# Two loads of 2 KB rows for the key and value weights, a first token block in column halves, and another order of value segments, in an attention and gated-MLP kernel

## The chip, the cores and the metric

The kernel runs on one core of one Trainium2 chip. The metric is the device time of one execution in microseconds (us). Before the change its median was 267.1 us. The five executions behind it lie between 266.8 and 267.2 us, so that an effect of half a microsecond is near the edge of what times alone can show. The profile's span (first to last instruction of the program) is about 2 us shorter than the device time.

PE is TensorE, PEld its weight loads, DVE is VectorE, ACT is ScalarE, POOL is GpSimd, SP is SyncE.

## The reference, cut to what matters

```python
def reference(A_x, A_wqkv, A_wo, B_x, B_w_gate, B_w_up, B_w_down):   # S = 2048, D = 512, F = 1792, bf16
    xn = _layernorm(A_x)
    # A: 32 heads of 16, causal sliding window of 256
    q, k, v = split(xn @ A_wqkv)
    p = softmax(where(mask, q @ k.T * Dh ** -0.5, -1e9))
    # B: (xn @ w_gate) * (xn @ w_up) @ w_down
    return A_x + (p @ v) @ A_wo + ((xn @ B_w_gate) * (xn @ B_w_up)) @ B_w_down
```

`B_x` isn't used. The work is cut into 4 chunks of 512 tokens, and a chunk into 4 token blocks of 128.

## The kernel before

The kernel plans itself: a small model in Python decides in which order instructions are issued and on which engine an evacuation runs; constants such as `land` and `wq` tell that model when loads land. They are not waits. In the traces each engine follows its list and waits on semaphores. An evacuation is the copy of a result of PE out of its accumulation memory; a load's landing is the time of the semaphore event that completes it.

The loads of the first chunk. Token block 0 comes from two queues, block 1 from ACT's, and then the weights in three loads of 512 KB each with rows of 1 KB: values, keys, queries.

```python
        load(nc.sync, self.x[0:64, 0, :], xv[0:64, 0, :])
        load(nc.scalar, self.x[64:128, 0, :], xv[64:128, 0, :])
        load(nc.scalar, self.x[:, 1, :], xv[:, 1, :])
        for n, lo in enumerate((1024, 512, 0)):
            load(nc.sync, self.Wqkv[:, :, lo:lo + 512], w["qkv"][:, :, lo:lo + 512])
            if n:
                load(nc.sync, self.x[:, n + 1, :], xv[:, n + 1, :])
        # ... then gate, up, the other tokens, down, output weights
```

A token block b of the first chunk goes: statistics (DVE), square root (ACT), reciprocal and "apply" (DVE), turn (four 128x128 transposes on PE), copy of the turned block to `xnT` (ACT or DVE), then projections on PE: values `v0.b`, keys `k0b<b>`, queries `q0b<b>`. PE's order before (warm-ups are matmuls on a constant whose results nobody reads; the gate group is the first work of part B):

```
42 warm-up matmuls, turn0, 6 warm-ups, v0.0, turn1, k0b0, k0b1, q0b0, q0b1, turn2, v0.1, v0.2, turn3, k0b2, q0b2, k0b3, q0b3, first gate group ...
```

The value groups (probabilities times values), 4 in each chunk. A segment is one strip of probabilities; each is eight small matmuls with 17 weight columns each, side by side in the array, which stream 64*m columns, m from 1 to 5. Long and short segments alternate:

```python
    def i_values(self, T, c, strips, banks):
        rest = sorted(((P, s) for P, batch in strips for s in batch), key=lambda x: -x[1][2])
        segments = []
        while rest:
            segments.append(rest.pop(0))
            if rest:
                segments.append(rest.pop())
        for n, (P, (k, q, m, at)) in enumerate(segments):
            # ... for lane in 2: for e in 4: one matmul of 64*m columns into banks[lane]
```

In chunks 1 to 3 that is m = 5,1,5,1,5,2,5,2,4,3,4,3 (96 matmuls), in chunk 0 it is 5,1,5,1,5,2,4,3,4 (72 matmuls).

The softmax here doesn't subtract the row's maximum and nothing guards it: scores larger than these inputs give would overflow.

## Time and profile before

| | before |
|---|---|
| median time | 267.1 us |
| span of the profile | 264.9 us |
| start to the first gate matmul | 17.51 us |
| from there to the end of the last vector addition | 244.44 us |
| from there to the end of the span | 3.00 us |

From the page of the kernel before: busy time and share, then busy tenths in 40 equal slices of the span, and what the DMA engines moved in each slice.

```profile
PE 260.4 (98%) x3458; PEld 131.0 (49%) x3458; DVE 190.1 (72%) x365; ACT 165.4 (62%) x122; POOL 119.2 (45%) x272
...
PE   8999999999999999999999999999999999999994
...
GB/s 188 373 374 351 226 43 0 4 2 0 4 2 32 90 22 24 0 2 2 2 0 42 83 22 20 0 6 0 2 2 22 21 22 22 0 2 0 2 2 80
```

PE is busy nearly always; the first slice (6.6 us) is the only one before the last that isn't full, and there the DMA engines move half of what they move in the next. Matmuls are pipelined and their ends modelled, so "busy" alone doesn't prove a limit. The waits of PE do (engine and line, what it waited for, us in total, times, longest; PEq is PE's own sequencer, at launch):

```profile
PE M L194 <- PEq L796: 0.8, 1, 0.8
PE M L669 <- ACT xnT L198: 0.2, 1, 0.2
```

Nothing else over 0.15 us in the whole program. The chain of waits of the first 20 us (start, us, what) is followed back from the end of that stretch ("issue" is time in which the profile shows nothing that was waited for):

```profile
0.84 4.64 PE M L194 x42
5.48 0.44 PE M L608 x4
5.92 0.02 issue
5.94 0.60 ACT xnT L198
6.55 0.04 issue
6.59 1.06 PE M L669 x16
7.66 0.33 PE M L608 x4
7.99 3.69 PE M L204 x64
```

Turn 0 at 5.3, its copy at 5.94, value projection 0 at 6.59, turn 1, then four projections of keys and queries without a gap. No DMA is in the chain. The landings, read from the trace's semaphore events: values 6.24 us, keys 7.73 (used at 7.82), queries 9.60 (used at about 9.7).

### The profile page before, as it was taken

What the parts mean: (1) busy time and instruction counts of PE and PEld (TensorE: products, weight loads), DVE (VectorE), ACT (ScalarE), POOL (GpSimd) and SP (SyncE); (2) the same over time, 40 slices, a digit from 0 to 9 for tenths busy, and PEclk for the clock granted to TensorE, in tenths of its full rate; (3) what the DMA queues carried; (4) which work ended last, traced back from release to release, by engine and by line L of the source; (5) the groups of instructions that cost most, each with busy time, mean ns of one, the idle gap of its engine ahead of it and who ended that gap; (6) DMA issues with size and microseconds to landing.
All of it is one profiled execution on the core that took longest, in us unless ns stands there. A gap on an engine that the chain in (4) does not pass through costs nothing.

```text
span 264.9 us, 7986 instructions
## 1 busy us (share of the span) xinstructions
PE 260.4 (98%) x3458; PEld 131.0 (49%) x3458; DVE 190.1 (72%) x365; ACT 165.4 (62%) x122; POOL 119.2 (45%) x272
## 2 busy tenths in 40 slices
PE   8999999999999999999999999999999999999994
PEld 8974444554445354464534353446544344544462
DVE  4889987888997629697996639796754449787404
ACT  3637676677677666777667676567886766673000
POOL 1404664554356463708256454718063545537000
PEclk9999999999999999999999999999999999999999
DMA  6999920000001300000001300000000000000002
GB/s 188 373 374 351 226 43 0 4 2 0 4 2 32 90 22 24 0 2 2 2 0 42 83 22 20 0 6 0 2 2 22 21 22 22 0 2 0 2 2 80
DMA packets 17251, 13.88 MB, mean 52 GB/s; under 512 B 7104, under 2 KB 17216, under 8 KB 17216
## 3 DMA queue, kind: packets, MB, share of 16 engines
q1 hardware_dynamic: 16848, 13.11, 17.3%
q8 instruction: 27, 0.44, 0.7%
q10 hardware_dynamic: 368, 0.26, 0.4%
q14 instruction: 8, 0.07, 0.1%
HBM read 9.70 MB, written 2.10 MB: 45 GB/s over the span
## 4 chain that ended last, share of the span: by engine, by line
PE 97%; DMA 1%; DVE 1%; ACT 0%; issue 0%
PE M L204 72%; PE S L212 9%; PE M L241 7%; PE M L669 6%; PE M L194 2%; DMA out_dram<-xn 1%; PE S L204 1%; DVE xn L762 1%; PE M L608 0%; ACT xnT L198 0%
## 5 line engine op out<-in xcount | busy, mean ns | idle before, releaser
L493 ACT ACTIVATE P<-S 128x2048 bf16<-128x2048 f32 x76 | 140.9, 1854 | 55.3 <-PE S L212 50.6
L221 POOL TENSOR_SCALAR_AFFINE_SELECT P<-P 64x256 bf16<-64x256 bf16 (+1 forms) x248 | 112.2, 455 | 117.4 <-ACT P L493 105.1
L204 PE MATMUL M<-xnT,Wg 128*128 128x512 bf16 x224 | 57.7, 380 | 0.0
L204 PE MATMUL M<-xnT,Wu 128*128 128x512 bf16 x224 | 57.7, 380 | 0.0
L204 PE MATMUL M<-Wd,hT 128*128 128x512 bf16 (+1 forms) x224 | 52.1, 373 | 0.0
L720 DVE TENSOR_TENSOR hT<-M,gsb 128x512 bf16<-128x512 f32 x56 | 38.2, 682 | 8.1 <-PE M L204 7.8
L204 PEld LDWEIGHTS <-hT 128*128 128x128 bf16 x238 | 21.7, 98 | 24.0 <-issue 2.8
L204 PEld LDWEIGHTS <-Wu 128*128 128x128 bf16 x224 | 20.5, 98 | 25.5 <-issue 2.8
L204 PEld LDWEIGHTS <-Wg 128*128 128x128 bf16 x224 | 20.1, 98 | 25.0 <-issue 3.5
L200 DVE CAST gsb<-M 128x512 bf16<-128x512 f32 x40 | 27.4, 686 | 5.3 <-PE M L204 5.0
L204 PE MATMUL M<-xnT,Wqkv 128*128 128x128 bf16 (+1 forms) x224 | 30.4, 288 | 0.0
L212 PE MATMUL S<-Q,K 32*128 32x320 bf16 (+3 forms) x720 | 30.0, 254 | 0.0
L227 DVE TENSOR_TENSOR P<-P,masks 128x512 int16<-128x512 int16 x56 | 22.6, 410 | 9.2 <-ACT P L493 9.2
L529 DVE STREAM_TRANSPOSE at<-M 128x512 f32<-128x512 f32 x32 | 21.4, 698 | 10.5 <-PE M L241 10.4
L212 PEld LDWEIGHTS <-K 32*128 32x128 bf16 x720 | 11.9, 92 | 32.3 <-issue 31.3
L280 DVE TENSOR_SCALAR K<-M,own 128x512 bf16<-128x512 f32 x28 | 20.0, 742 | 3.5 <-PE M L204 3.2
L204 PEld LDWEIGHTS <-Wqkv 128*128 128x128 bf16 x224 | 15.8, 98 | 10.8 <-issue 1.6
L241 PE MATMUL M<-P,V 64*17 64x320 bf16 (+4 forms) x1440 | 20.2, 252 | 0.0
L762 DVE TENSOR_TENSOR y<-M,x 128x512 bf16<-128x512 f32 x12 | 8.2, 684 | 15.0 <-PE M L204 14.9
L241 PEld LDWEIGHTS <-V 64*17 64x17 bf16 x1440 | 15.8, 85 | 2.8 <-issue 1.3
L204 PE MATMUL M<-Wo,OT 128*128 128x512 bf16 (+1 forms) x64 | 16.2, 374 | 0.0
L669 PE MATMUL M<-Wqkv,xnT 128*64 128x256 bf16 x256 | 15.7, 274 | 0.2 <-ACT xnT L198 0.2
(51 smaller groups left out, 136.2 us busy)
## 6 DMA issues: line engine op xcount, KB each, us to landing
Wg<-in_B_w_gate_dram SPq DMA_DIRECT2D x2, 896.0 KB, 10.3
Wu<-in_B_w_up_dram SPq DMA_DIRECT2D x2, 896.0 KB, 12.5
Wqkv<-in_A_wqkv_dram SPq DMA_DIRECT2D x3, 512.0 KB, 5.5
out_dram<-y SPq DMA_DIRECT2D x12, 128.0 KB, 1.7
x<-in_A_x_dram SPq DMA_DIRECT2D x1, 1024.0 KB, 14.3
Wd<-in_B_w_down_dram SPq DMA_DIRECT2D x2, 512.0 KB, 12.3
Wd<-in_B_w_down_dram SPq DMA_DIRECT2D x2, 384.0 KB, 8.5
x<-in_A_x_dram SPq DMA_DIRECT2D x1, 512.0 KB, 11.5
```

The lines of the kernel that those rows point to most:

```text
L200: self.nc.vector.tensor_copy(out=out, in_=in_)
L204: self.nc.tensor.matmul(ps, lhsT=a, rhs=b, start=first and n == 0, stop=last and n == len(pairs) - 1)
L212: self.nc.tensor.matmul(self.S[:, e, 64 * at:64 * (at + m)], lhsT=self.K[U % 3][rows, c, j].rearrange("p l t -> p (l t)"), rhs=self.Q[T % ...
L221: self.nc.gpsimd.affine_select(out=v, in_=v, pattern=[[0, 4], [0, n], [sign, 64]], base=0, fill=0.0, compare_op=ALU.is_gt if kind else ALU ...
L227: self.nc.vector.tensor_tensor(out=v, in0=v, in1=m, op=ALU.bitwise_and)
L241: self.nc.tensor.matmul(banks[lane][32 * e:32 * e + 17, 64 * q:64 * (q + m)], lhsT=self.V[U % 3][rows, j, 4 * c + e, 0:17], rhs=P[rows, e, ...
L280: self.nc.vector.tensor_scalar(out=out, in0=in_, scalar1=own, scalar2=None, op0=ALU.mult)
L493: ex = self.op(f"exp{g}", {"A": (took + 0.06, took + 0.18)}, [o], lambda e: self.nc.scalar.activation(out=P[:, :, 0:hi], in_=self.S[:, :, ...
L529: t = self.op(f"tr{v}", {"V": (0.63, 0.71)}, [o] + ts, lambda e, par=par: nc.vector.transpose(out=self.at[:, :, par, :], in_=self.M[banks[ ...
L669: self.nc.tensor.matmul(self.M[i][64 * lane:64 * lane + 64, 256 * jj:256 * jj + 256], lhsT=self.xnT[T % 2][:, k, tok], rhs=w[:, lane], sta ...
L720: x = self.op(f"u{T}.{f}", {"V": PSUM_COPY["V"]}, [o, ("gate", T, f)], lambda e: self.nc.vector.tensor_tensor(out=self.hT[T % 2][:, f, :], ...
L762: self.nc.vector.tensor_tensor(out=keep["y"][:, cols], in0=self.M[i][:, cols], in1=self.x[:, t, cols], op=ALU.add)
```

## The change

Its intent: get keys and values sooner by larger rows; start the first value projection on half of the columns while the other half is still being turned, copied and loaded; and order the value segments so that PE's instruction feed keeps up. The diff, cut to its core (a rank and the dependences that go with the halves are left out):

```diff
-    FIRST = True
+    FEED = 0.1
@@ loads
-        for n, lo in enumerate((1024, 512, 0)):
-            load(nc.sync, self.Wqkv[:, :, lo:lo + 512], w["qkv"][:, :, lo:lo + 512])
-            if n:
-                load(nc.sync, self.x[:, n + 1, :], xv[:, n + 1, :])
+        for k, cols in ((0, slice(512, 1536)), (2, slice(512, 1536))):
+            load(nc.sync, self.Wqkv[:, k:k + 2, cols], w["qkv"][:, k:k + 2, cols])
+        load(nc.sync, self.x[:, 2, :], xv[:, 2, :])
+        load(nc.sync, self.Wqkv[:, :, 0:512], w["qkv"][:, :, 0:512])
+        load(nc.sync, self.x[:, 3, :], xv[:, 3, :])
@@ value segments
-        rest = sorted(..., key=lambda x: -x[1][2])
-        segments = []
+        rest = sorted(..., key=lambda x: x[1][2])
+        keep, segments, t = rest.pop(0), [], 0.0
         while rest:
-            segments.append(rest.pop(0))
-            if rest:
-                segments.append(rest.pop())
+            fit = [n for n, x in enumerate(rest) if t + x[1][2] / 37.5 >= self.FEED * (len(segments) + 1)]
+            segments.append(rest.pop(fit[0] if fit else -1))
+            t += segments[-1][1][2] / 37.5
+        segments.append(keep)
@@ first chunk: what the planning model believes of the landings
-        land = (3.75, 3.9, 7.9, 9.8)
-        wv, wk, wq = 6.1, 7.4, 9.4
+        land = (3.6, 3.9, 7.3, 8.8)
+        wkv, wq = 6.3, 8.4
@@ block 0: apply, turn and copy in two column halves; 4 warm-ups after the turns, not 6
+            parts = 2 if b == 0 else 1
+            for n in range(parts):
+                cols = slice(n * 512 // parts, (n + 1) * 512 // parts)
 # ...
@@ value projection: weight rows outside, so that its first half needs rows 0 and 1 alone
-            for jj in range(2):
-                tok = slice(128 * b + 64 * jj, 128 * b + 64 * jj + 64)
-                for k in range(4):
+            for k in range(4):
+                for jj in range(2):
+                    tok = slice(128 * b + 64 * jj, 128 * b + 64 * jj + 64)
 # ... start=k + jj == 0, stop=k + jj == 4
```

With these constants the planner also gives PE another order in the first block:

```
... turn0 (two halves), 4 warm-ups, v0.0, k0b0, turn1, q0b0, k0b1, q0b1, turn2, ...
```

Value segments become 4,4,5,2,5,3,5,2,5,3,1,1 and, in chunk 0, 4,4,5,2,5,3,5,1,1.

More of the change, by code (lines that the diff above doesn't have):

```diff
@@ L229, in i_values @@
     def i_values(self, T, c, strips, banks):
-        rest = sorted(((P, s) for P, batch in strips for s in batch), key=lambda x: -x[1][2])
-        segments = []
+        rest = sorted(((P, s) for P, batch in strips for s in batch), key=lambda x: x[1][2])
+        keep, segments, t = rest.pop(0), [], 0.0
         while rest:
-            segments.append(rest.pop(0))
-            if rest:
-                segments.append(rest.pop())
+            fit = [n for n, x in enumerate(rest) if t + x[1][2] / 37.5 >= self.FEED * (len(segments) + 1)]
+            segments.append(rest.pop(fit[0] if fit else -1))
+            t += segments[-1][1][2] / 37.5
+        segments.append(keep)
         for n, (P, (k, q, m, at)) in enumerate(segments):
@@ L265, in i_root, with i_apply @@
                                      in1=self.mhalf[:, 0:n], op=ALU.pow)
-    def i_apply(self, t):
+    def i_apply(self, t, cols=slice(0, 512)):
         w, b = t // 4 % 2, t % 4
-        self.nc.vector.tensor_scalar(out=self.xn[b][:], in0=self.x[:, t, :], scalar1=self.mv[w][:, b, 0:1],
+        self.nc.vector.tensor_scalar(out=self.xn[b][:, cols], in0=self.x[:, t, cols], scalar1=self.mv[w][:, b, 0:1],
                                      scalar2=self.rs[w][:, b:b + 1], op0=ALU.subtract, op1=ALU.mult)
@@ L583, in bn @@
                 nc.vector.bn_aggr(out=self.mv[0][:, b, :], in_=keep["st"][:])
-            s = self.op(f"st{b}", {"V": (0.92, 0.94)}, [land[b]] + applied * (b == 1 and self.FIRST), bn, rank=3 + b)
+            s = self.op(f"st{b}", {"V": (0.92, 0.94)}, [land[b]] + applied * (b == 1), bn, rank=0.5)
             s = self.op(f"sq{b}", {"A": (0.20, 0.25)}, [s], lambda e, b=b: nc.scalar.activation(
@@ L590, in first_chunk @@
                 out=self.rs[0][:, b:b + 1], in_=self.ve[:, b:b + 1]), rank=0)
-            applied = [self.op(f"ap{b}", {"V": (0.38, 0.48)}, [s], lambda e, b=b: self.i_apply(b), rank=0)]
-            self.at_["ap", b] = applied[0]
-        self.op("table", {"A": (1.5, 1.5)}, roots, lambda e: nc.scalar.activation(
+            parts = 2 if b == 0 else 1
+            for n in range(parts):
+                cols = slice(n * 512 // parts, (n + 1) * 512 // parts)
+                took = (0.38, 0.48) if parts == 1 else (0.22, 0.30)
+                self.at_["ap", b, n] = self.op(f"ap{b}", {"V": took}, [s], lambda e, b=b, cols=cols: self.i_apply(b, cols), rank=0)
+            if b == 0:
+                applied = [self.at_["ap", 0, 1]]
+        self.op("table", {"A": (1.5, 1.5)}, roots + [("Q", 0, 0, 2)], lambda e: nc.scalar.activation(
             out=self.warm[:], in_=self.warm[:], func=ACT.Exp), rank=1)
-        last = self.op("masks", {"V": (0.15, 0.2)}, [self.at_["ap", 1]], lambda e: nc.vector.memset(self.masks[:], -1), rank=9)
+        last = self.op("masks", {"V": (0.15, 0.2)}, [self.at_["ap", 1, 0]], lambda e: nc.vector.memset(self.masks[:], -1), rank=9)
         for n in range(5):
@@ L603, in first_chunk, with turn, turned @@
             tok = slice(128 * b, 128 * b + 128)
-            ap = self.at_["ap", b]
-            def turn(i, b=b):
-                for k in range(4):
+            def turn(i, ks, b=b):
+                for k in ks:
                     self.nc.tensor.transpose(self.psT(i)[:, k, :], self.xn[b][:, 128 * k:128 * k + 128], self.ident[:])
                 if b == 0:
-                    self.keep_busy(6, 3)
-            def turned(o, i, b=b, tok=tok):
-                x = self.op(f"xT{b}", {"A": (0.48, 0.6), "V": (0.31, 0.41)}, [o],
-                            lambda e: self.copy(e, self.xnT[0][:, :, tok], self.psT(i)), rank=0)
+                    self.keep_busy(2 * ks[0], 3)
+            def turned(o, i, ks, b=b, tok=tok):
+                took = {"A": (0.48, 0.6), "V": (0.31, 0.41)} if len(ks) == 4 else {"A": (0.27, 0.38)}
+                ks = slice(ks[0], ks[-1] + 1)
+                x = self.op(f"xT{b}", took, [o], lambda e: self.copy(e, self.xnT[0][:, ks, tok], self.psT(i)[:, ks]), rank=0)
                 self.frees(x, i)
-                self.at_["xnT", 0, b] = x
+                self.at_["xnT", 0, b] = self.at_["xnT", 0, b, ks.start] = x
+                x.then.append(lambda o: self.at_.update({("begun", 0, b, ks.start): o.start}))
             def project(i, lo, tok=tok):
@@ L639, in first_chunk @@
             at = len(self.A) - 2 if b else 0
-            self.A.insert(at, Dense(f"turn{b}", 1.1, [ap], turn, turned))
-            self.add_v(0, b, wv)
-            self.add(f"k0b{b}", 4.2, [("xnT", 0, b), wk], lambda i, f=project: f(i, 512), k_out)
+            for n, ks in enumerate(([0, 1], [2, 3]) if b == 0 else ([0, 1, 2, 3],)):
+                self.A.insert(at + n, Dense(f"turn{b}", 1.1 * len(ks) / 4, [("ap", b, n)], lambda i, f=turn, ks=ks: f(i, ks),
+                                            lambda o, i, f=turned, ks=ks: f(o, i, ks)))
+            self.add_v(0, b, wkv - 0.6)
+            self.add(f"k0b{b}", 4.2, [("xnT", 0, b), wkv], lambda i, f=project: f(i, 512), k_out)
             self.add(f"q0b{b}", 4.2, [("xnT", 0, b), wq], lambda i, f=project: f(i, 0), q_out)
@@ L663, in emit @@
         def emit(i):
-            for jj in range(2):
-                tok = slice(128 * b + 64 * jj, 128 * b + 64 * jj + 64)
-                for k in range(4):
+            for k in range(4):
+                for jj in range(2):
+                    tok = slice(128 * b + 64 * jj, 128 * b + 64 * jj + 64)
                     w = self.Wqkv[:, k, 1024:1536].rearrange("p (h l d) -> p l h d", l=2, d=16)
@@ L669, in emit @@
                         self.nc.tensor.matmul(self.M[i][64 * lane:64 * lane + 64, 256 * jj:256 * jj + 256],
-                                              lhsT=self.xnT[T % 2][:, k, tok], rhs=w[:, lane], start=k == 0,
-                                              stop=k == 3, tile_position=(0, 64 * lane), skip_group_check=True)
+                                              lhsT=self.xnT[T % 2][:, k, tok], rhs=w[:, lane], start=k + jj == 0,
+                                              stop=k + jj == 4, tile_position=(0, 64 * lane), skip_group_check=True)
         def evac(o, i):
@@ L677, in evac @@
             self.at_["V", T, b] = x
-        self.add(f"v{T}.{b}", 4, [("xnT", T, b), land] + self.ring(T, 2)[:1 if T == 3 else 0], emit, evac, "C")
+        x = [("xnT", T, b)] if T + b else [("xnT", 0, 0, 0), ("begun", 0, 0, 2)]
+        self.add(f"v{T}.{b}", 4, x + [land] + self.ring(T, 2)[:1 if T == 3 else 0], emit, evac, "C")
     def add_qk(self, T, c):
```

## The prediction

> **What bounds the kernel.** TensorE. The page gives PE 260.4 us of a 264.9 us span (98%), PE is 97% of the chain of waits, and its only waits over 0.15 us are 0.8 us at launch and 0.2 us before the first value projection. From 6.59 to about 258.8 us PE always has a matmul in flight. So only two things can pay: real work starting before 6.59 us, and less time per PE group. The order of instructions, compared without lines and bank numbers, is the same in both programs after the first token block, apart from the value segments.
>
> **First block.** Before (timeline): 42 warm-up matmuls fill PE until 5.27 us, four turns start there, the ACT copy runs 5.94 to 6.54 (0.60), values start at 6.59, the next turn at 7.59. The weights landed at 6.24 (values), 7.73 (keys), 9.60 (queries). After:
> - The first apply, halved, ends near 5.0, but the turns still wait for the warm-ups at 5.27: nothing gained.
> - The first half copy can start near 5.70 and takes about 0.39 (estimate: 0.60 less half of the streaming). Values' first half starts near 6.1, its second near 6.5, once the second copy and rows 2, 3 of the weights are in. Gain about 0.45 us.
> - Loads: in the DMA view 1 KB packets take about 65 ns in the first microseconds and 45 ns from 6 us on. Rows of 2 KB halve the packets of 1 MB. "DMA: Bandwidth & Descriptors" of the Trainium skill (Why small descriptors are slow) gives a fixed cost per packet; this trace does not show what a 2 KB packet takes early. I take the new landing constants of the diff as a guess: keys and values near 6.5, queries near 8.6.
> - Then PE does key projection 0 (0.92), turn 1 (0.23) and reaches query projection 0 near 8.25, before its weights. I expect a new wait of 0.3 to 0.4 us there, which gives most of the 0.45 back. Net 0.1 to 0.45, taken as 0.25 us.
>
> **Value groups.** Each of the 12 groups with 96 matmuls takes 1.27 us up to the next group's start, of the 4 with 72 0.98 us (PE timeline). Streaming alone, 64 columns in about 28 ns, is 1.07 and 0.80. In the first 32 matmuls starts are 3 to 4 ns apart within a segment; the fifth segment's are 8 ns apart, its eighth 29 to 55 ns late, and this lag stays until the end. "TensorE: Matmul & The Clock Gate" (Architectural detail) gives a PE queue of 64, which is 32 pairs of load and matmul: it fits the place of the stall. Order 5,1,5,1 streams those 32 in 0.34 us, the new one (4,4,5,2,5,3,5,2,5,3,1,1) in 0.41 us, so the queue should be refilled in time. Estimate 0.03 to 0.06 us a group, 16 groups: 0.5 to 0.95, taken as 0.75 us.
>
> Value projections only swap loop order: 58 ns a matmul as before.
>
> **Prediction.** 267.1 - 0.25 - 0.75 = 266.1 us; 265.2 to 266.8. Faster by over 2%: 0.01; within 2%: 0.98; slower: 0.01.
>
> **What would show it.** Values from about 6.1 us; a PE wait for a DMA near 8.3 us; turn 2 at 11.1 to 11.4 instead of 11.51; value groups at about 1.21 and 0.93 us; dense groups unchanged (0.86 to 0.96); the tail after the last value group still about 19 us.
>
> **What would make it wrong.** 2 KB rows that land no earlier; the feed not limiting the groups; the PE clock rising later with fewer warm-ups; the score stage waiting for the query copy that moves from ACT to DVE.

## The result, and the profile after

267.0 us (266.92 to 267.61, 5 runs), against 267.1 us before. The ratio is 1.0006, with a 95% interval of 0.9991 to 1.0021. (A ratio here is the mean time of one kernel's runs over the mean of the other's runs of the same rounds, so not quite the ratio of the medians.) Executions over 1.5% slower than the fastest of the same kernel are left out of the means. A second series, 6 runs on another chip, gave 266.78 us against 267.34 and 0.9987 (0.9973 to 1.0000). So one series shows a loss of 0.16 us and the other a gain of 0.35 us, neither of them clear of nothing, where a gain of 1.0 us was predicted; the first lies just above the stated range of 265.2 to 266.8 us.

| part of the span, us | before | again | changed | again |
|---|---|---|---|---|
| start to the first gate matmul | 17.51 | 17.91 | 18.14 | 17.93 |
| to the last vector addition | 244.44 | 244.42 | 243.83 | 243.83 |
| to the end | 3.00 | 3.00 | 3.00 | 3.00 |

The middle part won 0.61 us and repeats within 20 ns. The start lost 0.63 us between the first traces; from trace to trace it varies by 0.4 us for before and by 0.2 us for the changed kernel.

The page of the changed kernel, lines as before:

```profile
PE 259.0 (98%) x3456; PEld 131.1 (49%) x3456; DVE 189.7 (72%) x367; ACT 165.0 (62%) x122; POOL 119.9 (45%) x272
...
PE   7899999999999999999999999999999999999994
...
GB/s 201 378 377 349 205 43 0 4 0 2 4 2 20 101 22 24 0 2 2 2 0 42 82 21 22 0 6 0 2 2 22 20 24 22 0 2 0 2 2 80
```

PE works 1.4 us less and is idle in the second slice too. The DMA engines moved 201 GB/s in the first slice, not 188: 7% more, no more than that. The waits of PE in the changed kernel:

```profile
PE M L679 <- DMA Wqkv<-in_A_wqkv_dram: 0.7, 1, 0.7
PE M L614 <- DVE xn L271: 0.6, 1, 0.6
PE M L205 <- DMA Wqkv<-in_A_wqkv_dram: 0.2, 1, 0.2
```

The DVE wait is the turns' for the apply; they begin at 5.27 us as before. The two waits for `Wqkv` are new: the second half of value projection 0 waits for the second load of keys and values, and query projection 0 for the query weights. PE's timeline (start, us, engine, line, operation, tiles, shape, count, and in brackets what ended the idle time before it):

```profile
6.03 0.63 PE L679 MATMUL M<-Wqkv,xnT 128*64 128x256 bf16 x8
7.37 0.63 PE L679 MATMUL M<-Wqkv,xnT 128*64 128x256 bf16 x8 [0.71 <-DMA Wqkv<-in_A_wqkv_dram]
7.93 1.07 PE L205 MATMUL M<-xnT,Wqkv 128*128 128x128 bf16 x16
8.84 0.39 PE L614 MATMUL M<-ident,xn 128*128 128x128 bf16 x4
9.46 2.85 PE L205 MATMUL M<-xnT,Wqkv 128*128 128x128 bf16 x48 [0.24 <-DMA Wqkv<-in_A_wqkv_dram]
```

The values did start at 6.03 us, 0.56 earlier. Their second half ran at 7.37, when the second load landed (7.33). So they end at 7.93, 0.34 later than before. And query projection 0, which is now one projection earlier in PE's order, met the landing of its weights (9.41). The chain of waits of the first 20 us now goes through that landing:

```profile
3.32 6.10 DMA Wqkv<-in_A_wqkv_dram
9.41 0.05 issue
9.46 2.85 PE M L205 x48
```

PE by stretches, before and then changed: us of the stretch, PE busy, count, PEld busy (the rest is DVE, ACT, POOL, clock, DMA share and GB/s).

```profile
6.59:17.51 10.92, 10.92 (x189) 10.34 (x190) 9.53 (x22) 5.71 (x11) 2.97 (x12) 1.00 1.07 372
17.51:261.95 244.44, 243.91 (x3221) 115.33 (x3218) 177.84 (x334) 157.23 (x107) 115.17 (x251) 1.00 0.13 34
```

```profile
6.03:18.14 12.11, 11.16 (x189) 10.32 (x189) 9.88 (x24) 5.60 (x11) 3.07 (x12) 1.00 1.06 378
18.14:261.97 243.83, 243.29 (x3221) 116.70 (x3218) 177.13 (x335) 157.14 (x108) 115.75 (x251) 1.00 0.12 33
```

From the first value matmul to the first gate matmul the same PE work took 10.92 us before, without idle time, and 12.11 us now. That is the whole loss: PE began the block 0.56 us earlier and ended it 0.63 us later. Counted from start to start, the two waits cost more than the 0.71 and 0.24 us in the brackets, which leave out the tail of the matmul before: the second half of the values starts 1.34 us after the first half (before 0.46), and query projection 0 starts 0.62 us after turn 1 (before, what follows turn 1 starts after 0.23). That is 0.88 and 0.39 us.

The gain, in one value group of chunk 2 (PE's timeline, before and then changed; the time to read is from the start of the 96 matmuls to the start of the next line):

```profile
156.97 1.34 PE L241 MATMUL M<-P,V 64*17 64x320 bf16 x96
158.24 0.60 PE L204 MATMUL M<-Wo,OT 128*128 128x512 bf16 x2
```

```profile
157.30 1.29 PE L243 MATMUL M<-P,V 64*17 64x256 bf16 x96
158.52 0.60 PE L205 MATMUL M<-Wo,OT 128*128 128x512 bf16 x2
```

It takes 1.27 us before and 1.22 us after. All 16 groups together: 19.116 us before, 18.520 after, so 0.596 us less; 11 of the 12 long ones went from 1.27 (the last one from 1.25) to 1.22, the four short ones from 0.976 to 0.943, and one became longer (1.270 to 1.295, in the same place in every trace of the new order). In that one the 96 matmuls start as in the others, the last at 1,098 ns; it is the projection after them that starts later, for a reason that I didn't find.

### The profile page after: what moved, and what is told of

It is laid out like the page before. It is cut to its first block, busy times and chain, and to the rows that moved or that the text cites. A ratio compares the mean times of both kernels' runs of the same rounds, so it can differ in the third digit from the quotient of the medians.

```text
span 265.0 us, 8000 instructions
## 1 busy us (share of the span) xinstructions
PE 259.0 (98%) x3456; PEld 131.1 (49%) x3456; DVE 189.7 (72%) x367; ACT 165.0 (62%) x122; POOL 119.9 (45%) x272
## 4 chain that ended last, share of the span: by engine, by line
PE 94%; DMA 3%; SPq 1%; DVE 1%; issue 0%
PE M L205 72%; PE S L213 9%; PE M L243 7%; PE M L679 5%; DMA Wqkv<-in_A_wqkv_dram 2%; SPq L148 1%; DMA out_dram<-xn 1%; PE S L205 1%; DVE xn L773 1%; PE M L614 0%
## 5 line engine op out<-in xcount | busy, mean ns | idle before, releaser
L205 PEld LDWEIGHTS <-Wqkv 128*128 128x128 bf16 x224 | 15.8, 98 | 11.1 <-issue 1.4
L243 PE MATMUL M<-P,V 64*17 64x320 bf16 (+4 forms) x1440 | 19.5, 252 | 0.0
L243 PEld LDWEIGHTS <-V 64*17 64x17 bf16 x1440 | 17.1, 86 | 2.8 <-issue 0.8
```

What stands on the lines that cost most here:

```text
L205: self.nc.tensor.matmul(ps, lhsT=a, rhs=b, start=first and n == 0, stop=last and n == len(pairs) - 1)
L243: self.nc.tensor.matmul(banks[lane][32 * e:32 * e + 17, 64 * q:64 * (q + m)], lhsT=self.V[U % 3][rows, j, 4 * c + e, 0:17], rhs=P[rows, e, ...
```

## The experiments

Theory: the value order gives its 0.6 us everywhere, and the first block loses as much because it is bound by the landing of weights, which 2 KB rows hardly bring forward, while PE now asks for them earlier or for more of them. Rivals: the gain in value groups is lost again later; the halves are at fault; the loads are harmless and only PE's order is wrong.

Two remarks on all runs. A few matmul records are missing in some traces (one of a group); where that touched a number, I allowed for 0.226 us, the time of the missing dense matmul. And for each run I give the three parts of the span as above.

### values_only: the value order alone

```diff
 (kernel before)
-        segments: longest and shortest in turn
+        segments: by feed, as in the changed kernel
```

> Kernel before with only the new order of value segments. Theory (the start took back what the value groups gave): the first block stays as before (first gate group at 17.5 us), the 12 groups of 96 take about 1.22 us instead of 1.27, the 4 of 72 about 0.94 instead of 0.98, time 0.6 us less than before: 266.5. Rival (PE time saved in value groups is lost again later in waits for ACT or DVE, so that the value order alone is worth nothing): 267.1, with new PE waits after 20 us.

Measured: 267.05 us median (266.55 to 267.16, 5 runs) against 267.12, ratio 0.9991 (0.9978 to 1.0003). Parts: 17.57, 243.86, 2.99 us. The spans of its 5 runs have a mean of 264.68 us, those of the 9 runs of before 265.21: 0.53 us less. The waits of PE show no new one in the middle. So the gain of the value groups is real, is kept, and doesn't depend on the rest; the rival falls. The device time shows only half of it, because what lies outside the span was 2.2 us in this kernel and 1.9 in before; no run explains that.

### loads_only: the loads alone

```diff
 (kernel before, its planning constants kept, so that PE's order is that of before)
-            load(nc.sync, self.Wqkv[:, :, lo:lo + 512], ...)      # values, keys, queries
+            load(nc.sync, self.Wqkv[:, k:k + 2, 512:1536], ...)   # keys and values, rows 0-1, rows 2-3; then queries
```

> Kernel before with only the new load instructions (keys and values in two loads of 2 KB rows, queries after); PE order, copies and value segments as before. Theory (the first value projection now needs all of the 1 MB of keys and values, and 2 KB rows land hardly earlier): first value matmul at about 7.4 us instead of 6.59, no other new wait, first gate group at about 18.3 us, time 0.75 us more: 267.9. Rival (the loads are harmless, the loss comes from the order in which PE now meets the query weights): at most 0.2 us more.

Measured: 267.82 us (267.53 to 269.45, 4 runs) against 267.12, ratio 1.0045 (1.0017 to 1.0073). Parts: 18.26, 244.44, 2.99. PE's timeline in this run:

```profile
6.69 0.47 PE L670 MATMUL M<-Wqkv,xnT 128*64 128x256 bf16 x4
7.57 0.84 PE L670 MATMUL M<-Wqkv,xnT 128*64 128x256 bf16 x12 [0.41 <-DMA Wqkv<-in_A_wqkv_dram]
8.35 0.40 PE L609 MATMUL M<-ident,xn 128*128 128x128 bf16 x4
8.58 3.85 PE L205 MATMUL M<-xnT,Wqkv 128*128 128x128 bf16 x64
```

As the theory said: three quarters of the first value projection wait for a load that brings keys that it doesn't need, landing at 7.53 us; the key projection starts 0.76 us later than before, and so does the gate (0.75). The loads by themselves are a loss of 0.75 us against the first trace of before, and of 0.59 us against the mean start of all its traces (17.67, below). The ratio says more than that because of one of the four executions, 269.45 us at a granted clock of 0.993; the other three have a mean of 267.72 us, 0.57 above before's 267.15.

### halves_old_loads: the halves alone

```diff
 (changed kernel: loads, constants and value segments of before; PE's order of the first block of before;
 the small pieces that go with the halves stay: 4 warm-ups, the rank of the statistics)
```

> Kernel before with only the column halves of the first block and the k-outer loop of the value projection; loads and value segments as before, PE's order in the first block held to that of before. Theory (with the old loads the next thing that ends the wait is the key weights at 7.73 us): values start at about 6.05 us and end near 7.1, then PE waits until about 7.75 for the key weights; first gate group at about 17.45 us, time within 0.1 us of before. Rival (the halves bring their 0.45 us where the loads are not in the way): first gate group at 17.05, time 266.65.

Measured: 266.63 us (266.57 to 267.08, 4 runs) against 267.12, ratio 0.9984 (0.9970 to 0.9997). Parts: 17.69, 244.44, 2.83; mean span 265.07 against 265.21. PE's timeline:

```profile
6.22 1.06 PE L682 MATMUL M<-Wqkv,xnT 128*64 128x256 bf16 x16
7.40 0.40 PE L617 MATMUL M<-ident,xn 128*128 128x128 bf16 x4
7.76 4.02 PE L204 MATMUL M<-xnT,Wqkv 128*128 128x128 bf16 x64
```

The values end earlier, and then PE waits for turn 1 and for the keys (7.72 us). The key projection starts at 7.76, against 7.82 before. The halves win nothing, because something else was due at the same time. The 64 matmuls of keys and queries took 0.17 us more, since the queries landed late here (9.78). The device time is 0.5 us shorter although the span is only 0.14 us shorter: again a difference outside the span, which I don't credit to the change.

### after_old_pe_order: the changed kernel with PE's old order

```diff
 (changed kernel)
-  v0.0 k0b0 turn1 q0b0 k0b1 q0b1 turn2
+  v0.0 turn1 k0b0 k0b1 q0b0 q0b1 turn2
```

> The changed kernel with PE's order in the first block held to that of before (turn 1 ahead of key projection 0, key projection 1 ahead of query projection 0). Theory: the wait for the second half of the key and value weights stays (values end at about 7.9 us), the wait for the query weights at 9.4 us goes; first gate group at about 17.85 us instead of 18.14, time 0.3 us less than the changed kernel: 266.75. Rival (all of the loss is the landing of keys and values): no gain, 267.0.

Measured: 266.92 us (266.82 to 268.74, 4 runs), ratio to before 1.0007 (0.9979 to 1.0035). Parts: 18.22, 243.98, 2.84. The number missed (17.85 expected), because in this trace the second load landed at 7.82 us and not 7.33. Its only new wait is for that load (1.0 us); the one for the queries is gone. Measured from the landing of the second load, the first gate matmul came 10.40 us later, against 10.81 in the changed kernel and 10.69 in its second trace: by this measure the order is worth 0.3 to 0.4 us, but one trace with a late landing hides it. The ratio is lifted by one of the four executions (268.74 us at a granted clock of 0.994). So with the wait for the queries gone, the wait for the second load ends the block.

### after_again and before_again: how much a trace can be trusted

```diff
 (both kernels, unedited)
```

> The changed kernel once more, unedited, to see how far its start varies. Theory: keys and values land between 7.3 and 7.8 us, the first gate group starts at 18.1 to 18.5 us, from there to the last vector addition 243.8 us; time within 0.2 us of before (266.9 to 267.3). Rival (the 18.14 us of its one trace was an unlucky landing): first gate group at 17.5, time 266.5.

> The kernel before once more, for a second trace of its start. Theory: values land at 6.1 to 6.3, keys at 7.7 to 7.9, first gate group at 17.5 to 17.8 us, from there to the last vector addition 244.4 us, from the last landing to the end 1.4 us.

after_again: 266.78 us (266.65 to 267.30, 6 runs) against 267.34, ratio 0.9987 (0.9973 to 1.0000); mean span 264.90 against 265.39. before_again: one run, 267.11 us. Both starts fell just outside what was expected (17.93 where 18.1 to 18.5 was, 17.91 where 17.5 to 17.8 was). Parts are in the table of the result. The landings of all traces with the loads of before and with two loads of 2 KB rows, in us:

```
                              values or first load   all keys and values    queries
1 KB rows  before                    6.24                  7.73               9.60
           before_again              6.51                  8.00               9.87
           values_only               6.27                  7.79               9.64
           halves_old_loads          6.18                  7.72               9.78
           segment_orders            6.11                  7.85               9.96
           values_two_wo_loads       6.28                  7.85               9.73
           mean                      6.27                  7.82               9.76
2 KB rows  changed                   5.83                  7.33               9.41
           after_again               5.56                  7.24               9.20
           loads_only                5.70                  7.53               9.62
           after_old_pe_order        5.90                  7.82               9.70
           no_half_wait              6.42                  7.78               9.64
           no_half_wait_old_order    5.70                  7.28               9.71
           mean                      5.85                  7.50               9.55
```

Rows of 2 KB bring the megabyte of keys and values 0.3 us sooner and the queries 0.2 us sooner; the planning constants of the change assumed 1.1 us (7.4 to 6.3) and 1.0 us (9.4 to 8.4). In the packets of the traces, 1,182 thousand bytes had moved by 6.5 us before and 1,257 after. The packets also say why it is so little: the median packet of 1 KB took 46 ns, that of 2 KB 84 ns, where two of 1 KB take 92. My estimate from these: 8 ns less for each of the 512 packets of 2 KB, on 16 engines, is 0.26 us. And the values as a whole, which land first in the old order (6.27), are now complete only with the keys (7.50): 1.2 us later.

The start of a kernel with before's first block had its first gate matmul at 17.51, 17.91, 17.57, 17.79 and 17.57 us (before, before_again, values_only, segment_orders, values_two_wo_loads; mean 17.67), the changed kernel at 18.14 and 17.93 (mean 18.04). On these means the loss of the start is 0.37 us rather than 0.63, and with the 0.6 us of the value groups some 0.2 us of gain remain, between the two series of times.

### no_half_wait and no_half_wait_old_order: which wait ends the block

Both are wrong: the second half of value projection 0 reads weight rows 0 and 1 again, which have landed, so that its wait goes and no race comes in. (The result differs from the reference by a relative error of 0.53.)

```diff
-                    w = self.Wqkv[:, k, 1024:1536].rearrange(...)
+                    w = self.Wqkv[:, k if T + b else k % 2, 1024:1536].rearrange(...)
```

> The changed kernel, wrong on purpose: the second half of the first value projection reads weight rows 0 and 1 again, which have landed, so that it does not wait for the second load. Theory (in the changed kernel's order it is the landing of the query weights that ends the last wait of the first block; in both of its traces the first gate group starts 8.7 us after query projection 0): values end near 7.1 us, key projection 0 starts when the second load lands, but query projection 0 still starts when the query weights land (9.2 to 9.7 us); first gate group 8.7 us after that, 17.9 to 18.4 us as without the edit. Rival (it is the wait for the second half, 0.6 to 0.7 us in the waits of PE, that delays the block): first gate group at 17.3 to 17.6 us.

> The same wrong edit in after_old_pe_order, where the first query projection comes a key projection later. Theory: the query weights no longer end the last wait; key projection 0 starts when the second load has landed (7.3 to 7.8 us), first gate group 9.8 us after that start, as in before (7.82 to 17.51 = 9.7): 17.1 to 17.6 us, so 0.5 us or more earlier than in the run without this edit, relative to the landing of the second load (there 10.4 us after it, here 9.85). Rival (the order does not matter): 18.0 us.

no_half_wait: 267.23 us (one run; before on the same chip 267.19). Parts: 18.37, 243.83, 3.00. PE's timeline:

```profile
7.46 1.32 PE L205 MATMUL M<-xnT,Wqkv 128*128 128x128 bf16 x16
8.62 0.39 PE L614 MATMUL M<-ident,xn 128*128 128x128 bf16 x4
9.68 2.85 PE L205 MATMUL M<-xnT,Wqkv 128*128 128x128 bf16 x48 [0.68 <-DMA Wqkv<-in_A_wqkv_dram]
```

With the first wait gone, the values were done by 7.46; but the query projection started at 9.68, after the landing at 9.64, and the first gate matmul came 8.69 us later. In the changed kernel's two traces it came 8.68 and 8.69 us after the query projection. So in the changed kernel the landing of the queries ends the last wait; the wait for the second load, three times as long in the waits of PE, was hidden in front of it. (In this trace the first load landed late too, at 6.42.)

no_half_wait_old_order takes both away: 266.90 us (one run). Parts: 18.09, 244.01, 2.83. The key projection started at 7.51 us, 0.3 earlier than in before, with the second load in at 7.28. But the first gate matmul was expected at 17.1 to 17.6 and came at 18.09. The waits of PE and a part of the chain of waits:

```profile
PE M L619 <- DVE xn L271: 0.6, 2, 0.3
PE M L205 <- DVE xnT L201: 0.3, 1, 0.3
```

```profile
10.06 0.70 DVE st L589
10.77 0.02 issue
10.79 0.18 DVE mv L590
10.97 0.05 DVE rs L596
11.02 0.65 DVE K L282
11.67 0.33 DVE xn L271
12.00 0.05 issue
12.05 0.40 PE M L619 x4
```

My theory of two waits was one short. With no weight in the way, PE ran ahead into DVE: key projection 1 waited for the copy of turn 1, and turn 2 for the apply of block 2. DVE had taken the statistics of block 3 first (at 10.06 us, just when that block landed, 10.04), then a key evacuation, and only then the apply that PE waited for. The change gives those statistics a higher rank in the planner than before, so this order may be its own doing; no run takes that apart. Three things come due within a few tenths of a microsecond here: the keys, the queries and DVE's work for the next blocks.

### after_values_first, after_values_first_x1, values_first_x1_again: values ahead of keys in the second load

```diff
 (changed kernel with PE's old order)
-   load rows 2-3 of keys and values (2 KB rows)
+   load rows 2-3 of values, then rows 2-3 of keys (1 KB rows)
 (the two _x1 runs also:)
-   block 1: ScalarE's queue, beside the weights
+   block 1: SyncE's queue, ahead of the weights
```

> The changed kernel with the second load of 2 KB rows split into two of 1 KB rows, values ahead of keys, and PE's order in the first block held to that of before. Theory (the loss is that the first value projection waits for keys that it does not use): its second half starts at about 6.7 us instead of 7.4, ends near 7.2; key projection 0 starts when the keys land, about 7.6; first gate group at about 17.4 us against 18.14 in the changed kernel, time 0.7 us less than that: 266.4. Rival (the loss comes from the halves or from 2 KB rows as such): first gate group still at or above 18.0.

> The run after_values_first again, with the load of token block 1 issued by SyncE ahead of the weights, not by ScalarE beside them: in after_values_first that block landed at 5.95 us (3.75 in the changed kernel) because its issue lost to the weights', and turn 1 had to wait for it. Theory as there: second half of the first value projection at about 6.9 us, turn 1 near 7.4, keys used from about 7.8, first gate group near 17.5 against 18.14 in the changed kernel. Rival (splitting the keys from the values in the loads does not help): 18.0 or later.

> after_values_first_x1 again, since its only trace fell in a slow execution. Theory as there: second half of the first value projection at about 6.9 us, turn 1 near 7.4, key projection 0 from about 7.75 when the keys land, first gate group near 17.5 to 17.6 us. Rival (splitting keys from values does not help): 18.0 or later. Three fast executions had spans of 264.7 to 265.1, which favours something between.

after_values_first: 266.98 us (4 runs), ratio 1.0002 (0.9989 to 1.0016); parts 18.06, 243.98, 2.60. The values ran through early (from 5.98), but turn 1 ran at 7.92: block 1 had landed at 5.95 us, not at 3.75. The cause shows in the issues. ScalarE issues block 1 at 1.39 to 1.42 us, SyncE the first weights at 1.44. In 10 traces ScalarE's issue ended by 2.00 us and the block landed at 3.6 to 4.6 us; in 5 traces SyncE's ended first (2.0) and ScalarE's at 2.1 to 2.3, and the block landed at 5.9 to 6.2, behind the weights. after_again is among those 5 and the changed kernel's first trace among the 10, so it is chance of the execution and not of the program. Two of the six traces with 2 KB rows in the table of landings are among the 5 (after_again, no_half_wait); without them the means of keys and queries are 7.49 and 9.61, so that the comparison stands.

after_values_first_x1's profile fell in a slow execution (374.7 us, granted clock 0.66); its three fast runs had spans of 264.7 to 265.1 us and a ratio of 0.9993 (0.9979 to 1.0008). The repeat, values_first_x1_again: 266.89 us (4 runs), ratio 0.9986 (0.9972 to 1.0000); parts 18.31, 243.83, 2.57. It fell short again. Issued after block 1, the weights landed later (first load 6.55, values 7.28, keys 7.96), so that the values began at 6.59 as in before, and key projection 1 then waited 0.5 us for a copy on DVE. Splitting values from keys removes the wait it aims at and meets the next. This rules out an easy repair, not the theory.

### split_keys_1k, split_keys_2k and three variants: an attempt to beat both

```diff
 (halves, new value segments)
+   keys in two loads of rows 0-1 and 2-3; key projection 0 in two parts that use them
+   PE: v0.0, k0b0 first half, turn1, k0b0 second half, k0b1, v0.1, q0b0, turn2, q0b1, ...
    1k: values as one load of 1 KB rows;  2k: rows 0-1 of keys and values as one load of 2 KB rows
    _x1: block 1 on SyncE ahead of the weights;  _xq: block 0 whole on SyncE, block 1 whole on ScalarE, both first
```

> Aimed at beating both. New value segments and column halves; loads of 1 KB rows as before, but the keys in two loads; key projection 0 split by those halves, its first half filling the wait for the second; value projection 1 ahead of query projection 0, so that no wait for the query weights is left. Theory: values at 6.1, first half of the keys near 7.1, second half at 7.8, no PE wait over 0.2 us after 6.1; first gate group at about 17.1 us; time 267.1 less 0.4 less 0.6 = 266.1. If the start can't be won because bytes land no sooner, 17.5 and 266.5.

> As the run before it, but the first half (rows 0 and 1) of keys and values in one load of 2 KB rows, then values, then keys of the second half. Theory: as before it, first gate group 17.0 to 17.2, time 266.1; the landing of the keys matters less here since half of the key projection can run from about 6.7 us on. If 2 KB rows land later than 1 KB rows in front of them: 17.3 and 266.3.

> split_keys_1k with token block 1 loaded by SyncE ahead of the weights. Theory (its start was held up by token block 1 landing at 6.2 us, so that turn 1 ran at 8.2): block 1 lands before 4.6, values from 6.1, turn 1 near 7.7, key projection 1 near 8.6; first gate group at 17.3 instead of 18.18, time 0.8 us less: 265.7. Rival (block 1 was not what held it up): 18.0 and 266.4.

> split_keys_2k with token block 1 loaded by SyncE ahead of the weights. Theory: as split_keys_1k_x1; weights up to 0.3 us later than in split_keys_2k since their issue starts 0.5 us later; first gate group near 17.3, time 265.7. Rival: 18.0 and 266.3.

> split_keys_2k with token block 0 whole by SyncE and block 1 whole by ScalarE, both issued first, so that neither can lose to the weights. Theory: block 1 lands before 4.6; weights as in split_keys_2k; block 0 may land 0.2 us later than the 3.1 us of before, which would shift the values by as much; first gate group 17.3 to 17.5, time 265.8.

| run | median us (runs) | before | ratio (95%) | parts of the profiled run |
|---|---|---|---|---|
| split_keys_1k | 266.45 (5) | 266.96 | 0.9975 (0.9961 to 0.9988) | 18.18, 243.83, 2.61 |
| split_keys_2k | 266.30 (5) | 266.96 | 0.9981 (0.9968 to 0.9994) | 18.19, 243.83, 2.56 |
| split_keys_1k_x1 | 266.60 (5) | 267.06 | 0.9988 (0.9976 to 1.0001) | 17.88, 243.99, 2.54 |
| split_keys_2k_x1 | 266.87 (5, one slow) | 267.06 | 0.9988 (0.9975 to 1.0001) | profile in a slow execution, 517 us |
| split_keys_2k_xq | 266.68 (6) | 267.06 | 0.9986 (0.9971 to 1.0000) | 18.27, 243.98, 2.48 |

None got its first gate matmul to the 17.0 to 17.5 us that I expected. In the first two, block 1 landed at 6.2 and 6.1 us; in the third it landed at 3.79, turn 1 ran at 7.80 and the next limit was the copy of that turn (0.2 us) and a later landing of the values (6.30, a wait of 0.4). These are versions with the gain of the value groups, a start no better than before's, and an end that is 0.4 to 0.5 us shorter.

That shorter end has nothing to do with the change. In before, the changed kernel and values_only, 1.4 us pass from the landing of the last output to the end of the span; in the split kernels 0.9, as in the two values-first kernels (1.0). In before SyncE then stands still for 0.5 us between its last wait (263.57) and its drain (264.07); in the split kernels a stall of that length falls into the wait for the output itself.

### values_two_wo_loads: is that stall a matter of how many instructions SyncE has?

```diff
 (values_only)
-        load(nc.sync, self.Wo[:], w["o"])
+        load(nc.sync, self.Wo[:, 0:2], w["o"][:, 0:2])
+        load(nc.sync, self.Wo[:, 2:4], w["o"][:, 2:4])
```

> values_only with the load of Wo issued as two, which PE needs only after 85 us: one more instruction on SyncE and nothing else. It tests why the split kernels were shorter than their first gate group allows: from the last landing to the end of the span takes 1.4 us in before, the changed kernel and values_only, but 0.9 in those with more loads on SyncE, where a stall of 0.5 us of SyncE's own falls into the wait for the output. Theory (the place of that stall hangs on how many instructions SyncE has): first gate group 17.6, last addition at 261.4, then 0.9 us instead of 1.4 from landing to end; span 263.9 to 264.4, 0.4 us less than values_only. Rival (chance of an execution): 1.4 us, span as values_only.

Measured: 266.90 us (266.58 to 267.04, 5 runs) against 267.34, ratio 0.9983 (0.9971 to 0.9996). Parts: 17.57, 243.90, 2.96; 1.36 us from the last landing to the end. One more instruction doesn't move the stall: my theory falls, and why the split kernels end sooner stays open. The run is useful in another way: it is the value order alone once more, on another chip, and clear of before by its interval: mean span 264.62 against 265.39.

### segment_orders: why the value groups got shorter

```diff
 (kernel before; another order for each of the four groups of a chunk; groups of 96 / of 72)
+  (a) 4,4,5,2,5,3,1,5,5,1,2,3 / 4,4,5,2,5,1,5,1,3     well fed, long end
+  (b) 1,2,1,2,5,5,5,5,4,4,3,3 / 1,2,1,3,5,5,5,4,4     short beginning
+  (c) as before
+  (d) 5,5,5,5,4,4,3,3,2,2,1,1 / 5,5,5,4,4,3,2,1,1     short end
```

> Kernel before, but each of the four value groups of a chunk has another order of segments. Theory ([...] a segment can only be fed about 0.06 us after the segment four places earlier has ended, so it is the first four, and any four in a row, that must be long enough; the length of the last segment does not matter). Rival (it is the short last segments that made the groups shorter). Groups of 96, to the next group's start: (a) 4,4,5,2,5,3,1,5,5,1,2,3, fed well but a long end: theory 1.22 to 1.24, rival 1.27. (b) 1,2,1,2,5,5,5,5,4,4,3,3: theory 1.30 or more, rival 1.27. (c) as before: 1.27 in both. (d) 5,5,5,5,4,4,3,3,2,2,1,1, short end but fed late there: theory 1.27 to 1.30, rival 1.22. Groups of 72: (a) 0.95, (b) 1.00, (c) 0.98, (d) 1.00 by the theory.

Measured (one look), us to the next group's start, groups of 96 and of 72:

| | theory | rival | measured |
|---|---|---|---|
| (a) | 1.22 to 1.24, 0.95 | 1.27 | 1.26, 0.995 |
| (b) | 1.30 or more, 1.00 | 1.27 | 1.30, 1.003 |
| (c) | 1.27, 0.98 | 1.27 | 1.27, 0.975 |
| (d) | 1.27 to 1.30, 1.00 | 1.22 | 1.30, 1.048 |

The order (d) ends on the shortest segments and is, with (b), the slowest, so it isn't the short end that helps. But (a) missed the theory's range and came out near the rival's number; the starts below show that it wasn't fed as well as I had thought. The starts of the first and the eighth matmul of a segment, in ns from the group's start, show where each order loses time (read from the trace, groups of 96):

```
segment         1        2        3        4        5        6        7        8        9       10       11        12
before       0..23  141..165 170..193 306..330 335..413 471..527 532..603 663..719 724..793 828..902 910..985 1020..1094
changed      0..23  115..138 224..247 360..383 415..439 551..575 634..657 770..793 852..875 988..1011 1044..1067 1072..1098
(a)          0..24  115..139 225..248 360..384 416..440 552..575 635..658 663..725 800..864 935..975 983..1020 1024..1085
(b)          0..23   34..56   91..113 119..143 222..281 357..419 492..555 627..691 762..826 871..936 981..1045 1063..1127
(d)          0..23  142..164 278..300 414..436 550..571 659..681 768..790 851..872 933..955 989..1014 1045..1096 1121..1179
```

A segment's eight matmuls start within 21 to 26 ns when they have been fed; when they haven't, they are spread over 37 to 80 ns. Before, that happens at segment 5; in (b) at segment 5, where it begins 103 ns after segment 4, not 55 as a fed one does after a segment of that length (4 to 5 in the changed order); in (a) from segment 8 on, behind a segment of length 1; in (d) only at segments 11 and 12, at the end of a row of short ones; in the changed order nowhere. A rival is that the loading of weights itself is the limit. The traces speak against it: in the early segments the weight loads start 3 to 4 ns apart, in the late ones 8 to 9 ns apart, so they could go faster. What hands them on so slowly isn't shown directly; a queue that is refilled at that pace is my reading. "TensorE: Matmul & The Clock Gate" of the Trainium skill (Architectural detail) gives a PE queue of 64 with a partial reorder window, and 64 entries are 32 pairs of weight load and matmul, four segments; the traces agree on the place, since the first late start is never before segment 5. My estimate that a segment is fed 0.06 us after the segment four places earlier has ended placed (b) and the long (d) right; it gave (a) 0.02 to 0.05 and the short (d) 0.05 us too little.

## Why the prediction was wrong, point by point

- "TensorE" as the bound and no slack elsewhere in the middle: right. The middle part fell by what the value groups won (0.61 against 0.596 us), and values_only kept it.
- "Value groups ... 0.5 to 0.95, taken as 0.75 us": right in mechanism and within its range, 0.60 us. The groups came to 1.223 and 0.943 us, forecast at about 1.21 and 0.93, and one of the 16 got longer. segment_orders supports the feed as the cause and rejects the short end. (The sum of streaming doesn't follow from its own 28 ns: the segments of a long group add up to 40, which gives 1.12 us and not 1.07.)
- "The turns still wait for the warm-ups at 5.27: nothing gained": the start at 5.27 was right in both traces, but in the first for another reason: its warm-ups ended at 4.64 us and the turns waited 0.6 us for the first half of the apply, which ended at 5.21 and not near 5.0. In after_again the reason was as forecast: the last warm-up started at 5.17 us, the turns at 5.27.
- "Values' first half starts near 6.1": right, 6.03 and 6.10 us. "Its second near 6.5": wrong, 7.37 and 7.28.
- "I take the new landing constants of the diff as a guess: keys and values near 6.5, queries near 8.6": this is the step that failed. They landed at 7.33 and 9.41 us (7.24 and 9.20 in the second trace). The constants said what the planner believes, and I let them stand in for a measurement that the trace of before could have bounded. By 7.73 us its DMA engines had moved all that lies ahead of the end of the keys, 1.31 MB; at the 373 GB/s of the second slice, 1.2 us are 0.45 MB, a third of it. The only room was in the first slice, at 188 GB/s, and it became 201; the first 2.1 of its 6.6 us pass before the first packet moves. How this ends in a loss: the change puts query projection 0 one projection earlier in PE's order, and the first gate matmul follows its start by 8.68 us (before 7.78). With the queries at 9.41 that gives 18.14 us. With the landings of the forecast (6.5 and 8.6) it would have been about 17.33 (estimate: 8.6, 0.05 from landing to start, 8.68), close to the 17.26 that the forecast gain of 0.25 us means. So the rest of the forecast's sum about held, and the landings were what it had wrong.
- "A new wait of 0.3 to 0.4 us ... which gives most of the 0.45 back": the place was right (query projection 0) and the size too, 0.39 us from start to start (0.26 in after_again; 0.24 in the waits of PE), though at 9.1 to 9.4 us and not near 8.3; but it came after a second wait, of 0.71 us, that I had not counted since the landing was misjudged.
- The term of the sum that was mis-sized is thus "Net 0.1 to 0.45, taken as 0.25 us" of gain in the first block: it was a loss, 0.63 us between the first traces and 0.37 us on the means of all traces. Turn 2, named as a sign at 11.1 to 11.4 us, came at 12.15 and 11.94.
- The tail and the dense groups were unchanged, as forecast (19.0 us after the start of the last value group; 0.86 to 0.96 us).
- "What would make it wrong" named this cause first: "2 KB rows that land no earlier". Named, but not weighed: the low end of the range for the first block was a gain of 0.1 us, though a landing as of before in the new order of loads meant a loss.
- Not foreseen at all: that the first block has three limits within a few tenths of a microsecond (keys, queries, DVE's work for the next blocks), so that no single repair moved its end before 17.5 us.

What stays open: why the split kernels end 0.5 us sooner, why one value group got longer, and why what lies outside the span differs between kernels (1.7 us in halves_old_loads, 1.9 in before, 2.2 in values_only). On these runs I would choose the value order alone with the old start, though times alone hardly set it apart from the changed kernel (mean span 264.62 against 264.90 us in the one series that has both, 5 and 6 executions): values_only and values_two_wo_loads won 0.5 and 0.8 us of span against before in their own series. split_keys_1k measured fastest by its ratio (0.9975, 0.5 us by the medians), but part of that is the shorter end, which I can't explain and wouldn't build on.

## What to carry to other kernels

When several loads feed one stretch, first ask which bytes are in front of the ones that are needed: merging two loads to get larger rows delays the part that was needed first until the last byte of the other. Constants in a planner or a scheduler are beliefs; check them against the landings and against bytes over measured rate before a prediction, or a new instruction order, rests on them. Where small matmuls come in packs, look at the starts within a pack: in this kernel packs came late behind runs of short ones, and an order that avoids this won 0.05 us in a group of 1.27 us.

## What the Trainium skill lacked or had wrong

- "DMA: Bandwidth & Descriptors", Why small descriptors are slow: the example that it works out for the fixed cost per packet is one of 256 bytes; what is lacking is the size at the rows of this case, a median of 46 ns for 1 KB and 84 ns for 2 KB (0.3 us gained over 1.31 MB). It also lacks the slow beginning of a program: the first issue starts at 0.80 us, no packet moves before 2.1 us, and then it is 164 to 221 GB/s up to 4 us, 299 to 383 from 4 to 6 us and 362 to 374 from 6 to 8 us, in six traces with either row size.
- "DMA: Bandwidth & Descriptors", Issuing engines are not separate DMA queues: it says that issuing from several engines only saves sequencer time. Here it also made an order uncertain: a 128 KB load that ScalarE began to issue some 0.03 us ahead of SyncE's weights landed at 3.6 to 4.6 us in 10 traces and at 5.9 to 6.2 in 5.
- "TensorE: Matmul & The Clock Gate", Architectural detail: the queue of 64 is there, but not when a place comes free. In before and segment_orders packs of eight matmuls came late behind runs of short ones, with a weight load and a matmul every 8 to 9 ns: up to 1.30 us for a group, against 1.22 in the changed order, where none came late.
- The pages give times for what the runtime puts around a program, but none has the program's own end: 2.5 to 3.0 us from the last vector addition to the last instruction, of which 0.9 to 1.4 us follow the landing of the last output, differing between kernels for a reason that these runs don't show.
